# Sigmoid attention and a split-precision MLP on one core: attention issued in held groups of two pieces, with small moves at the start

## The chip, the cores and the metric

The kernel runs on one core of a Trainium2 chip. The time is device microseconds for one execution; before the change three runs gave a median of 1160.83 us (1160.44 to 1162.7). One further execution was recorded by the hardware profiler, and all durations below come from it.

## The reference, cut to what matters

```python
scores = q @ k.T / sqrt(64) - log(448)          # 8 batches x 12 heads, 448 x 448
x = (1 / (1 + exp(-scores))) @ v                # sigmoid attention, no row sum
x = x.transpose(0, 2, 1, 3).reshape(3584, 768)
h = x @ w_in                                    # 768 -> 2048
g = where(h >= 1, h, where(h <= -1, 0, (h + 1) ** 2 / 4))
out = g @ w_out                                 # 2048 -> 768
```

q, k and v are float32, the two weights float64.

## The kernel before, in words

**Precision.** Nearly every product is done with float16 halves: an operand is scaled by a power of two and split into a high half (ACT, or POOL) and a low half (DVE, or POOL: what the high half missed), and three matmuls add high x high, low x high and high x low in PSUM. The first eight pairs of heads go through in plain float32 instead.

**Attention.** The unit is a pair of heads (6 pairs a batch, 48 in all), and a pair has four pieces: three of 128 keys and a middle one with the last 64 keys of both heads (`NPC` pieces, piece number `i`, pair `p`, place `c`). A piece has two halves. `scores` makes the scores of some pieces in PSUM tiles `psc` (two buffers, `ps_sc`): for float16 pairs two full-array matmuls on 128 rows per piece (L409), then two matmuls on 64 rows each, one for each head, which the array runs at the same time in its two row halves (L418). The middle piece of pairs 14 and later has three full-array matmuls in their place (L404). `weigh` then takes the sigmoid on ACT (L447 for the first 14 pairs, L450 later) and splits it into halves `ahl` on ACT (L458) and DVE (L459). `av` multiplies by v (L491): each matmul fills 64 columns, one head each, and two run at the same time in the array's two column halves; a piece has six of them, a middle one four. So three ways of dividing the array alternate on PE: whole, two row halves (scores' second part), two column halves (av).

**The MLP.** `up` (batches 0 and 1, L719) and `up_blocks` (later batches, L685, with seven block products from pre-mixed weights) make h; `bend` does the activation on ACT and DVE; `down` (L755) makes the output. All are full-array matmuls. They are emitted as a list of units, and `step(i)`, which emits pieces of attention of the next batch, is called between units at even shares, so attention of batch b+1 lies among the MLP of batch b. `step` emits the scores some pieces ahead and then `av`: one piece at a time for pairs before 14, and from pair 14 on two pieces at every even place.

**What sets the order.** The program is written in that order, but only SP's queue keeps it. On the other engines a scheduler moves instructions: it takes the ready instruction of the highest priority by its own estimate, so two matmuls of one piece may end up apart with MLP matmuls between them. PE works strictly through the order that comes out.

**The start.** SP loads pair 0 (L307: q and k in one transfer, L308: v), then a chunk of w_in (L210), and so on. Until about 67 us PE does the float32 attention of pairs 0 to 7 while ACT (L236) and DVE convert the sixteen chunks of w_in. `find_scale` at step 12 finds the scale of the first eight chunks; `split(0)` and `split(1)` (L277 on ACT, L280 on DVE) follow at once, `split(2)` and `split(3)` after batch 0's x is done. `prep_a` (largest values, L335) and `prep_b` (halves, L366 and L367, and their transfers L380/L381) prepare the first two float16 pairs, 8 and 9, at steps 19 and 22, 20 and 23. `all_sum` (L155) is a tiny matmul that adds up largest values for the preparation two pairs ahead.

Of the kernel before, what the change touches and what calls it, by code (L numbers as in the profile page):

```python
# [14 lines left out]
F32 = mybir.dt.float32  # L15
# [23 lines left out]
WI_A = 12  # L39
WO_A = 42  # L40
# [15 lines left out]
CORN = 10  # L56
TP = 1
# [12 lines left out]
def sigmoid_attention_mlp(ctx: ExitStack, tc: tile.TileContext, first_qvk, qkv, w_in, w_out, out_t):  # L70
# [117 lines left out]
    class Weight:  # L188
# [84 lines left out]
        def split(self, f):  # L273
# [4 lines left out]
            if self is wi and f > AHEAD:  # L278
                behind(ins, "g")
# [22 lines left out]
    def load_pair(p):  # L302
        if p >= NPAIR or not first_time("load", p):
            return
        if p < NFULL:
            r = full[:, slot_of(p)]
            nc.sync.dma_start(out=r[:, ::2, :], in_=first_qvk[p, :, ::2, :])  # L307
            nc.sync.dma_start(out=r[:, 1, :], in_=first_qvk[p, :, 1, :])  # L308
            ready[p] = r, r[:, 1]
            return  # L310
# [74 lines left out]

    def scores(todo):

        tiles = []
        for i in todo:
# [5 lines left out]
            if p < NFULL:  # L395
                r = ready[p][0]
                for j in range(2):
                    out = psc[j * D : (j + 1) * D, 0, :S] if mid else psc[:, j, :S]
                    rows = slice(j * D, (j + 1) * D)
                    nc.tensor.matmul(out, r[rows, 2, w], r[rows, 0, :], start=True, stop=True)  # L400
            elif mid and p >= NFULL + NHALF:
                hl = ready[p][4]
                for t, (kh, qh) in enumerate(((0, 0), (1, 0), (0, 1))):
                    nc.tensor.matmul(psc[:, 0, :S], corner(p)[:, kh, :], hl[:, 0, qh, :], start=t == 0, stop=t == 2)  # L404
            else:
                kq = ready[p][0]
                for j in range(2):
                    out = psc[j * D : (j + 1) * D, 0, :S] if mid else psc[:, j, :S]
                    nc.tensor.matmul(out, kq[:, j, 1, w], kq[:, j, 0, :], start=True, stop=False)  # L409
        for i, psc in zip(todo, tiles):  # L410
# [8 lines left out]
            if mid and p >= NFULL + NHALF and p + 2 in maxes:  # L419

                sums[p + 2] = all_sum(maxes[p + 2], 3, psc[:, 1, :])
# [16 lines left out]
    def weigh(i, psc):  # L438
# [6 lines left out]
        if p < NFULL + NHALF:  # L445
            a32 = att_p.tile([P, 2, S], F32, tag="ahl", name="a32")
            nc.scalar.activation(a32[:, :n, :], a, AF.Sigmoid, bias=nls, scale=sqk)  # L447
# [9 lines left out]
        for x, hi, lo in parts:  # L457
            nc.scalar.activation(hi, x, AF.Copy, scale=ATT)  # L458
            nc.vector.scalar_tensor_tensor(out=lo, in0=x, scalar=ATT, in1=hi, op0=ALU.mult, op1=ALU.subtract)  # L459
# [4 lines left out]
    def av(i):  # L464
        p, c = divmod(i, NPC)
        b, hp = divmod(p, NP)
        if c == 0:
            state["pav"] = ps_av.tile([P, 512], F32, tag="pav", name="pav")
            if hp == 0:
                state["xm"] = sml_p.tile([P, NP], F32, tag="xm", name="xm", bufs=2)  # L470
        pav = state["pav"]
        at = pieces.pop(i)
        mid = c == NKC
        v = ready[p][1]
        split = p >= NFULL + NHALF
        terms = []
        for j in range(2):
            o = slice(j * D, (j + 1) * D)
            full_v = slice((2 * c + j) * D, (2 * c + j + 1) * D)
            if p < NFULL and mid:  # L480
                full_v = slice(2 * c * D, (2 * c + 1) * D)
            if not split:
# [487 lines left out]
```

## Time and profile before

| what | value |
|---|---|
| median of three runs | 1160.83 us |
| profiled execution | 1159.12 us, span of its instructions 1157.4 us |
| PE busy | 1135.0 us, 7662 matmuls |
| DVE, ACT, POOL busy | 815.8, 722.1, 294.4 us |
| granted TensorE clock | 0.999 |

The profile page lists, by engine, how long instructions were under way. A matmul's own duration overlaps that of the next (they are pipelined), so what a matmul costs PE is read from the starts: from its start to the start of the one behind it. In the timeline view like instructions in a row are merged: `start, duration, engine, line, operation, out<-in, array rows*columns, shape, count`. The field such as `64*128` names the part of the array that a matmul uses. A bracket at a row's end is the engine's idle time before it and what ended that.

### The profile page before, as it was taken

The numbers are of one execution on the slowest core, as the hardware profiler recorded it, in microseconds if no ns is written. First come the engines' busy times: TensorE is split into PE (matmuls) and PEld (weight loads), VectorE is DVE, ScalarE is ACT, GpSimd is POOL, SyncE is SP. The second block draws the span as 40 slices with busy tenths as digits, with TensorE's granted clock in tenths as the row PEclk, the third lists the DMA queues.
The fourth block names the chain that finished last, engine by engine and source line by source line (L and its number), as shares of the span: only waits on it lengthen the run. The fifth ranks groups of instructions, "written<-read, shape, count | busy, mean of one in ns | idle before, by whom it ended". The sixth has DMA issues, their size and how long they took to land.

```text
span 1157.4 us, 20215 instructions
## 1 busy us (share of the span) xinstructions
PE 1135.0 (98%) x7662; PEld 666.1 (58%) x7662; DVE 815.8 (70%) x1730; ACT 722.1 (62%) x1199; POOL 294.4 (25%) x367
## 2 busy tenths in 40 slices
PE   8899999999999999999999999999999999999998
PEld 2234334444446775567745785457854677558954
DVE  6988886879987895468936787367964589646820
ACT  6978888578666784557754786447764576423410
POOL 0000000001542354324523353325344233210000
PEclk9999999999999999999999999999999999999999
DMA  9943443162564654225632465224742165203300
GB/s 366 380 138 135 143 165 97 50 212 105 192 209 144 239 211 127 76 94 205 219 102 65 145 207 203 66 66 147 264 145 76 53 207 200 100 17 123 133 22 27
DMA packets 58112, 170.00 MB, mean 147 GB/s; under 512 B 8608, under 2 KB 39840, under 8 KB 51872
## 3 DMA queue, kind: packets, MB, share of 16 engines
q1 hardware_dynamic: 56288, 159.29, 39.9%
q10 hardware_dynamic: 1728, 9.44, 2.3%
q8 instruction: 60, 0.98, 0.3%
q14 instruction: 36, 0.29, 0.1%
HBM read 126.94 MB, written 23.40 MB: 130 GB/s over the span
## 4 chain that ended last, share of the span: by engine, by line
PE 76%; DMA 8%; DVE 6%; ACT 4%; POOL 3%; issue 1%; SPq 0%; POOLq 0%; DVEq 0%; ACTq 0%
PE po L755 30%; PE ph L685 23%; PE pav L491 8%; PE ph L719 7%; DMA raw<-qkv 4%; PE psc L409 3%; PE psc L418 3%; DMA w_out_sb<-w_in 2%; PE psc L404 1%; DVE ahl L459 1%; ACT psc L450 1%; POOL hl L373 1%; DVE mixa L625 1%; ACT dump L335 1%; POOL raw L371 1%
## 5 line engine op out<-in xcount | busy, mean ns | idle before, releaser
L755 PE MATMUL po<-ghl,w_out_sb 128*128 128x448 f16 x2304 | 446.9, 353 | 1.8 <-ACT ghl L735 1.8
L755 PEld LDWEIGHTS <-w_out_sb 128*128 128x128 f16 x2304 | 221.5, 98 | 217.2 <-issue 17.6
L685 PE MATMUL ph<-w_in_sb 128*128 128x224 f16 x3024 | 307.7, 259 | 1.7 <-DMA w_in_sb<-blocks 1.3
L685 PEld LDWEIGHTS <-w_in_sb 128*128 128x128 f16 x3024 | 282.6, 98 | 31.1 <-issue 27.6
L459 DVE SCALAR_TENSOR_TENSOR ahl<-psc,ahl 128x896 f16<-128x896 f32 (+1 forms) x170 | 153.0, 900 | 98.8 <-ACT ahl L458 96.9
L450 ACT ACTIVATE psc<-psc,nls,sqk 128x896 f32<-128x896 f32 (+1 forms) x136 | 129.8, 971 | 94.0 <-PE psc L418 76.1
L371 POOL TENSOR_SCALAR raw<-raw,qkv_s 128x448 f32<-128x448 f32 (+1 forms) x93 | 70.9, 777 | 443.8 <-DVE qkv_i L135 355.7
L458 ACT ACTIVATE ahl<-psc 128x896 f16<-128x896 f32 (+1 forms) x170 | 127.0, 762 | 30.6 <-DVE ahl L459 29.4
L719 PE MATMUL ph<-xhl,w_in_sb 128*128 128x448 f16 x576 | 112.5, 353 | 0.0
L335 ACT ACTIVATE dump<-raw 128x448 f16<-128x448 f32 (+1 forms) x105 | 61.6, 587 | 72.0 <-DMA raw<-qkv 71.3
L694 DVE TENSOR_TENSOR xhl<-ph,xhl 128x224 f32<-128x224 f32 x240 | 87.7, 383 | 26.0 <-PE ph L685 19.6
L491 PE MATMUL pav<-ahl,v 128*64 128x448 f16 x748 | 98.2, 360 | 0.4 <-DVE ahl L459 0.4
L735 ACT ACTIVATE ghl<-g 128x448 f16<-128x448 f32 x128 | 72.5, 572 | 37.2 <-DVE g L734 36.7
L732 ACT ACTIVATE g<-xhl,hr,ihr 128x448 f32<-128x448 f32 x96 | 68.7, 752 | 41.8 <-DVE xhl L694 40.8
L736 DVE TENSOR_TENSOR ghl<-g,ghl 128x448 f16<-128x448 f32 x128 | 84.2, 664 | 8.2 <-ACT ghl L735 7.7
L733 DVE SCALAR_TENSOR_TENSOR g<-g,rk 128x448 f32<-128x448 f32 x112 | 79.8, 727 | 13.9 <-ACT g L732 13.5
L719 PEld LDWEIGHTS <-w_in_sb 128*128 128x128 f16 x576 | 54.8, 98 | 58.2 <-issue 8.9
L373 POOL TENSOR_TENSOR hl<-raw,hl 128x448 f16<-128x448 f32 x62 | 72.8, 1194 | 0.0
L409 PE MATMUL psc<-qk 128*128 128x448 f16 x252 | 66.4, 354 | 2.8 <-ACT a L447 1.8
L734 DVE SCALAR_TENSOR_TENSOR g<-xhl,ihs,g 128x448 f32<-128x448 f32 x96 | 66.3, 708 | 0.3
L768 DVE TENSOR_SCALAR o<-po,od 128x448 f32<-128x448 f32 x42 | 28.5, 679 | 53.1 <-PE po L755 53.1
L430 POOL COPY w_in_sb<-hl 64x128 f16<-64x128 f16 x68 | 32.4, 476 | 127.3 <-DVE hl L367 125.4
(151 smaller groups left out, 1131.6 us busy)
## 6 DMA issues: line engine op xcount, KB each, us to landing
w_in_sb<-blocks SPq DMA_DIRECT2D x48, 1344.0 KB, 6.6
raw<-qkv SPq DMA_DIRECT2D x34, 704.0 KB, 4.8
qk<-hl SPq DMA_DIRECT2D x320, 56.0 KB, 2.0
w_out_sb<-w_in SPq DMA_DIRECT2D x16, 768.0 KB, 11.1
out_t<-o SPq DMA_DIRECT2D x48, 224.0 KB, 1.9
blocks<-mixs SPq DMA_DIRECT2D x8, 768.0 KB, 3.5
w_out_sb<-w_out ACTq DMA_DIRECT2D x6, 768.0 KB, 4.6
raww<-w_out ACTq DMA_DIRECT2D x6, 768.0 KB, 5.8
```

Of the source, the lines that this page charges most:

```text
L371: nc.gpsimd.tensor_scalar(out=rt, in0=rt, scalar1=s[:, t : t + 1], scalar2=1.0, op0=ALU.mult, op1=ALU.mult)
L373: nc.gpsimd.tensor_tensor(out=dst[:, 1, :], in0=rt, in1=hi, op=ALU.subtract)
L409: nc.tensor.matmul(out, kq[:, j, 1, w], kq[:, j, 0, :], start=True, stop=False)
L450: nc.scalar.activation(a, a, AF.Sigmoid, bias=nls, scale=sqk)
L458: nc.scalar.activation(hi, x, AF.Copy, scale=ATT)
L459: nc.vector.scalar_tensor_tensor(out=lo, in0=x, scalar=ATT, in1=hi, op0=ALU.mult, op1=ALU.subtract)
L491: nc.tensor.matmul(pav[j * D : (j + 1) * D, :S], *terms[j][t], start=c == 0 and t == 0, stop=mid and t == len(terms[j]) - 1,)
L685: nc.tensor.matmul(out, w[:, wt, wh, c * P : (c + 1) * P], xc[:, xt, c, xh, :], start=j in (0, 2) and c + wh + xh == 0, stop=c == HC - 1 a ...
L694: add = lambda out, q, other: nc.vector.tensor_tensor(out=out, in0=quarter(q), in1=other, op=ALU.add)
L719: nc.tensor.matmul(ph[:, :S], w_in_sb[:, f, wh, c * P : (c + 1) * P], xhl[:, c, xh, :], start=c == 0 and wh + xh == 0, stop=c == NCC - 1 a ...
L736: (nc.gpsimd if f % GPOOL else nc.vector).tensor_tensor(out=ghl[:, f, 1, :], in0=g, in1=hi, op=ALU.subtract)
L755: nc.tensor.matmul(po[:, :S], w_out_sb[:, f, wh, m * P : (m + 1) * P], ghl[:, f, gh, :], start=f == lo and wh + gh == 0, stop=f == hi - 1 ...
```

## The change

It has five parts.

1. **Held groups.** `weigh` notes the instructions that make a piece's operands (`made`). The first matmul of a call of `scores` now waits for those of the pieces two before (whose PSUM tiles it takes over), and the first matmul of a call of `av` waits for all the pieces of the call. Until then no matmul of that group is ready for the scheduler, and afterwards all are.
2. **Two pieces from pair 7 on.** `step` emits pieces in twos from pair 7 (`GROUPED`), not from pair 14. `av` takes the list.
3. **Order in `scores`.** The half with j=1 of L409 comes first, and `all_sum` stands between the whole-array and the row-half matmuls of the group, not behind them.
4. **The first transfer is divided.** q, then the first 128 columns of k, then the rest of k.
5. **Later splits and preparation.** `split(0)`, `split(1)` and `split(2)` come at steps 21, 23 and 24, `split(3)` after x; pair 9's preparation is left to the ordinary call at steps 28 and 30, and pair 8's `prep_b` comes at step 21.

```diff
+    made = {}
+    def when_made(some):
+        waits = [ins for i in some for ins in made.get(i, ())]
+        def once(ins):
+            while waits:
+                tc.add_manual_dep(ins.ins, waits.pop().ins.name, ...)
+        return once
     def scores(todo):
+        once = when_made(i - 2 for i in todo)
...
-                for j in range(2):
+                for j in (1, 0):
-                    nc.tensor.matmul(out, kq[:, j, 1, w], kq[:, j, 0, :], start=True, stop=False)
+                    once(nc.tensor.matmul(out, kq[:, j, 1, w], kq[:, j, 0, :], start=True, stop=False))
+        for i, psc in zip(todo, tiles):
+            p, c = divmod(i, NPC)
+            if c == NKC and p >= NFULL + NHALF and p + 2 in maxes:
+                sums[p + 2] = all_sum(maxes[p + 2], 3, psc[:, 1, :])
...
-    def av(i):
+    def av(some):
+        once = when_made(some)
+        for i in some:
...
-        if i < NPC * (NFULL + NHALF):
+        if i < NPC * GROUPED:
             more, some = i + LAG + 1, [i]
...
-            nc.sync.dma_start(out=r[:, ::2, :], in_=first_qvk[p, :, ::2, :])
+            if p == 0:
+                nc.sync.dma_start(out=r[:, 0, :], in_=first_qvk[p, :, 0, :])
+                for w in (slice(0, P), slice(P, S)):
+                    nc.sync.dma_start(out=r[:, 2, w], in_=first_qvk[p, :, 2, w])
...
-            for what, when in ((load_pair, L0), (prep_a, A0), (prep_b, A0 + 1)):
-                for k in range(2):
+            for what, when in ((load_pair, L0), (prep_a, A0), (prep_b, A0 + 2)):
+                for k in range(1 if what != load_pair else 2):
...
-                    wi.split(0)
-                    wi.split(1)
+            if at in SPLITS:
+                with tc.high_priority(offset=WI_PRIO):
+                    wi.split(SPLITS.index(at))
```

The order that the scheduler makes of it differs all along PE. PE's queue in batch 2's first block products shows how; `psc` with its number is the PSUM tile of one piece, `qk` and `hl` are the stacked and the plain halves of q and k. Before:

```order
L409 LDWEIGHTS qk_4923
L409 MATMUL psc_5328<-qk_4923 128x448
L418 LDWEIGHTS hl_4912
L418 MATMUL psc_5328<-hl_4912 128x448
L418 LDWEIGHTS hl_4912
L418 MATMUL psc_5328<-hl_4912 128x448
L409 LDWEIGHTS qk_4923
L409 MATMUL psc_5331<-qk_4923 128x448
L409 LDWEIGHTS qk_4923
L409 MATMUL psc_5331<-qk_4923 128x448
L418 LDWEIGHTS hl_4912
L418 MATMUL psc_5331<-hl_4912 128x448
```

The same two pieces after the change, whose lines L435 and L449 are L409 and L418 of before:

```order
L435 LDWEIGHTS qk_4925
L435 MATMUL psc_5333<-qk_4925 128x448
L435 LDWEIGHTS qk_4925
L435 MATMUL psc_5333<-qk_4925 128x448
L449 LDWEIGHTS hl_4914
L449 MATMUL psc_5330<-hl_4914 128x448
L449 LDWEIGHTS hl_4914
L449 MATMUL psc_5330<-hl_4914 128x448
L449 LDWEIGHTS hl_4914
L449 MATMUL psc_5333<-hl_4914 128x448
L449 LDWEIGHTS hl_4914
L449 MATMUL psc_5333<-hl_4914 128x448
```

The whole-array matmuls of both pieces now stand together, and so do the row-half ones, so that the array is divided anew once for two pieces.

ACT's queue from the first piece of pair 6 on, in the float32 attention (`a` is a piece's sigmoid, with `nls` its bias; `hl` the halves of pair 8, and with `hl,m` the largest values of pair 9). Before:

```order
L277 ACTIVATE w_in_sb<-w_in_sb,wi_s 128x768
L447 ACTIVATE a_440<-psc,nls 128x896
L335 ACTIVATE hl,m_444<-raw 128x448
L366 ACTIVATE hl<-raw,qkv_s 128x448 x2
L236 ACTIVATE w_in_sb<-w_out_sb 128x768
L335 ACTIVATE hl,m_444<-raw 128x448
L236 ACTIVATE w_in_sb<-w_out_sb 128x768
L447 ACTIVATE a_455<-psc,nls 128x896
L497 ACTIVATE x_92<-pav 128x448
L447 ACTIVATE a_488<-psc,nls 128x896
L447 ACTIVATE a_661<-psc,nls 128x448
L366 ACTIVATE hl<-raw,qkv_s 128x448 x2
```

After, where L475, L238, L376, L279 and L530 are L447, L236, L366, L277 and L497 of before:

```order
L475 ACTIVATE a_440<-psc,nls 128x896
L238 ACTIVATE w_in_sb<-w_out_sb 128x768
L376 ACTIVATE hl<-raw,qkv_s 128x448 x2
L279 ACTIVATE w_in_sb<-w_in_sb,wi_s 128x768
L475 ACTIVATE a_451<-psc,nls 128x896
L530 ACTIVATE x_92<-pav 128x448
L475 ACTIVATE a_460<-psc,nls 128x896
L279 ACTIVATE w_in_sb<-w_in_sb,wi_s 128x768
L475 ACTIVATE a_633<-psc,nls 128x448
L279 ACTIVATE w_in_sb<-w_in_sb,wi_s 128x768
L475 ACTIVATE a_660<-psc,nls 128x896
L475 ACTIVATE a_688<-psc,nls 128x896
```

Pair 9's two L335 and two L366 are gone from here, and the splits L279 stand between the sigmoids of pair 6 one by one.

SP's queue at the start (`ghl` is the buffer of the float32 pairs, `first_qvk` their data). Before:

```order
L307 DMA ghl<-first_qvk 128x2x448
L308 DMA ghl<-first_qvk 128x448
L210 DMA w_out_sb<-w_in 128x1536
L307 DMA ghl<-first_qvk 128x2x448
L308 DMA ghl<-first_qvk 128x448
```

After:

```order
L313 DMA ghl<-first_qvk 128x448
L315 DMA ghl<-first_qvk 128x128
L315 DMA ghl<-first_qvk 128x320
L318 DMA ghl<-first_qvk 128x448
L212 DMA w_out_sb<-w_in 128x1536
L317 DMA ghl<-first_qvk 128x2x448
```

Two issues more stand ahead of v, and the rest of k moves behind the first 128 columns. POOL's queue is the same in both.

More of the change, by code (lines that the diff above doesn't have):

```diff
@@ L399, in scores @@
                     rows = slice(j * D, (j + 1) * D)
-                    nc.tensor.matmul(out, r[rows, 2, w], r[rows, 0, :], start=True, stop=True)
+                    once(nc.tensor.matmul(out, r[rows, 2, w], r[rows, 0, :], start=True, stop=True))
             elif mid and p >= NFULL + NHALF:
@@ L458, in weigh @@
             nc.scalar.activation(hi, x, AF.Copy, scale=ATT)
-            nc.vector.scalar_tensor_tensor(out=lo, in0=x, scalar=ATT, in1=hi, op0=ALU.mult, op1=ALU.subtract)
+            made.setdefault(i, []).append(nc.vector.scalar_tensor_tensor(
+                out=lo, in0=x, scalar=ATT, in1=hi, op0=ALU.mult, op1=ALU.subtract
+            ))
         pieces[i] = ahl
     state = {"scored": 0}
-    def av(i):
[L465 to L482, printed above, removed]
-                r = o if mid else slice(0, P)
-                terms.append([(v[r, full_v], at[r, 0 if mid else j, :])])
-            elif mid:
-                terms.append([(v[:, vh, full_v], at[:, 0, j, :]) for vh in range(2)])
-            else:
-                terms.append([(v[:, vh, full_v], at[:, ah, j, :]) for vh, ah in ((0, 0), (1, 0), (0, 1))])
-        for t in range(len(terms[0])):
-            for j in range(2):
-                nc.tensor.matmul(
-                    pav[j * D : (j + 1) * D, :S], *terms[j][t],
-                    start=c == 0 and t == 0, stop=mid and t == len(terms[j]) - 1,
-                )
@@ new lines, in av @@
+    def av(some):
+        once = when_made(some)
+        for i in some:
+            p, c = divmod(i, NPC)
+            b, hp = divmod(p, NP)
+            if c == 0:
+                state["pav"] = ps_av.tile([P, 512], F32, tag="pav", name="pav")
+                if hp == 0:
+                    state["xm"] = sml_p.tile([P, NP], F32, tag="xm", name="xm", bufs=2)
+            pav = state["pav"]
+            at = pieces.pop(i)
+            mid = c == NKC
+            v = ready[p][1]
+            split = p >= NFULL + NHALF
+            terms = []
+            for j in range(2):
+                o = slice(j * D, (j + 1) * D)
+                full_v = slice((2 * c + j) * D, (2 * c + j + 1) * D)
+                if p < NFULL and mid:
+                    full_v = slice(2 * c * D, (2 * c + 1) * D)
+                if not split:
+                    r = o if mid else slice(0, P)
+                    terms.append([(v[r, full_v], at[r, 0 if mid else j, :])])
+                elif mid:
+                    terms.append([(v[:, vh, full_v], at[:, 0, j, :]) for vh in range(2)])
+                else:
+                    terms.append([(v[:, vh, full_v], at[:, ah, j, :]) for vh, ah in ((0, 0), (1, 0), (0, 1))])
+            for t in range(len(terms[0])):
+                for j in range(2):
+                    once(nc.tensor.matmul(
+                        pav[j * D : (j + 1) * D, :S], *terms[j][t],
+                        start=c == 0 and t == 0, stop=mid and t == len(terms[j]) - 1,
+                    ))
@@ L854, in sigmoid_attention_mlp @@
         group_scales(0, inv_x, 0)
-    wi.split(2)
-    wi.split(3)
+    for f in range(len(SPLITS), AHEAD + 1):
+        wi.split(f)
     units = ups(0) + downs(0, 0)
```

24 lines of the change are left out of this document (16 added, 8 removed).

## Prediction

> **What bounds the kernel now.** The page comes first: it says which engine has no room.
>
> ```profile
> span 1157.4 us, 20215 instructions
> PE 1135.0 (98%) x7662; PEld 666.1 (58%) x7662; DVE 815.8 (70%) x1730; ACT 722.1 (62%) x1199; POOL 294.4 (25%) x367
> ```
>
> PE is under way for all but 22 us. So either PE's waits go, or its matmuls must take less time. The list of waits on PE shows what the first can give:
>
> ```profile
> PE psc L400 <- DMA ghl<-first_qvk: 4.4, 1, 4.4
> PE psc L400 <- ACT a L447: 3.6, 6, 1.3
> PE psc L171 <- DVE diag L161: 2.1, 1, 2.1
> PE po L755 <- ACT ghl L735: 1.8, 3, 1.1
> PE psc L409 <- ACT a L447: 1.8, 3, 1.0
> ```
>
> The first two, 8 us, lie in the float32 attention ahead of 67 us; the rest are single events. The larger stock is inside "busy", and only starts show it. PE's timeline in one batch's block products:
>
> ```profile
> 500.21 1.32 PE L491 MATMUL pav<-ahl,v 128*64 128x448 f16 x12
> 501.46 6.21 PE L685 MATMUL ph<-w_in_sb 128*128 128x224 f16 x63
> 507.51 0.54 PE L409 MATMUL psc<-qk 128*128 128x448 f16 x2
> 507.99 0.36 PE L418 MATMUL psc<-hl 64*128 64x448 f16 x2
> 508.28 0.55 PE L409 MATMUL psc<-qk 128*128 128x448 f16 x2
> 508.77 0.36 PE L418 MATMUL psc<-hl 64*128 64x448 f16 x2
> 509.06 1.14 PE L491 MATMUL pav<-ahl,v 128*64 128x448 f16 x10
> 510.13 4.49 PE L685 MATMUL ph<-w_in_sb 128*128 128x224 f16 x45
> ...
> 523.92 1.89 PE L685 MATMUL ph<-w_in_sb 128*128 128x224 f16 x18
> 525.65 0.73 PE L409 MATMUL psc<-qk 128*128 128x448 f16 x3
> 526.31 0.55 PE L418 MATMUL psc<-hl 64*128 64x448 f16 x4
> 526.79 0.95 PE L491 MATMUL pav<-ahl,v 128*64 128x448 f16 x8
> ...
> 541.96 0.36 PE L418 MATMUL psc<-hl 64*128 64x448 f16 x1
> 542.26 1.90 PE L685 MATMUL ph<-w_in_sb 128*128 128x224 f16 x18
> ```
>
> The field 128\*128, 64\*128 or 128\*64 says how the array is divided. I read four prices from start to start.
>
> - Six pairs of L491 take 501.46 - 500.21 = 1.25 us, five take 510.13 - 509.06 = 1.07. One pair more is 0.18 to 0.19 (I use 0.19), so a run of L491 costs 0.12 us beside its pairs, until what is behind it starts.
> - Two L418 side by side take 508.28 - 507.99 = 0.29, two such pairs 526.79 - 526.31 = 0.48: 0.19 a pair and 0.10 a run.
> - A single L418 takes 542.26 - 541.96 = 0.30, as much as two: a pair that is torn apart pays its 0.19 twice.
> - Going over from the whole array to a divided one: two L409 take 507.99 - 507.51 = 0.48 ahead of L418, and three take 526.31 - 525.65 = 0.66. Three at 0.19 are 0.57, two are 0.38; so about 0.10 is the change. Where the array stays whole nothing is added: 18 L685 take 525.65 - 523.92 = 1.73, or 0.096 each, with L409 behind them.
>
> So each change of the array's division costs PE about 0.1 us that shows as busy, not as idle.
>
> [...]
>
> **The change part by part.** *Held groups, pieces in twos, the order in scores* act as one: they decide how often PE's queue changes its division. I counted that in the order of both programs; the held first matmul makes it come out so, since all of a group becomes ready at once.
>
> - Runs of float16 L491: 126 before (48 of odd length, each with a torn pair's half), 86 after (16 odd). 40 runs fewer by 0.12 is 4.8 us; 16 pairs mended (32 odd runs fewer, two to a pair) by 0.19 is 3.0.
> - Runs of L418: 122 (20 of one matmul) to 91 (2 of one). 31 by 0.10 is 3.2; 9 pairs mended by 0.19 is 1.7.
> - Entries from the whole array into a divided one: 178 to 95. 83 by 0.096 is 8.0.
>
> Together 20.7 us: 4.8 of them before the first block product, 15.9 in batches 2 to 6. The float32 part hardly changes (99 changes of division with a float32 side before, 97 after), and I put it at nothing. PE has no other work to hide these under, and it waits for nobody meanwhile, so each is on the path.
>
> *The moved `all_sum`* is inside that count: it stood behind L418 and made the array whole once more. *The reversed j* moves no cost: the same two matmuls in the other order; if it cost anything it would be one 0.10 per scores group at most, and the rows have no sign of it.
>
> *What holding adds.* The waiting instruction is the first matmul of a group, and PE takes its queue in order: all MLP matmuls behind it wait too, then `bend` on ACT and DVE. What is the cover? In the new order 63 to 81 L685 or some 40 to 50 L755 stand between groups; in the block products the shortest way is a run of 12 L491 (1.25) and 63 L685 (6.05), 7.3 us from the last L418 to the next scores. What is needed: the second piece's low half, which frees its PSUM tile.
>
> ```profile
> 531.25 1.08 DVE L459 SCALAR_TENSOR_TENSOR ahl<-psc,ahl 128x896 f16<-128x896 f32 x1
> ```
>
> Its piece was in the run of four L418 that ended at 526.31 + 0.55 = 526.86, and the row ends at 532.33: 5.5 us. That leaves 1.8 us. But ACT and DVE are not empty there:
>
> ```profile
> 140.00:160.00 20.00, 19.36 (x102) 8.38 (x101) 18.83 (x39) 18.47 (x29) 0.00 (x0) 1.00 0.42 122
> 501.00:573.00 72.00, 72.00 (x645) 55.40 (x642) 60.25 (x129) 56.83 (x102) 33.07 (x41) 1.00 0.54 189
> ```
>
> (PE, PEld, DVE, ACT, POOL busy.) DVE has 60.25 of 72 us in the block products and 18.83 of 20 at 140 us. Bounds: nothing, if the margin holds everywhere; 12 us, if one group in each of nine loaded places (five batches, four in batches 0 and 1) waits as long as the longest wait for a sigmoid above, 1.3. I take 2.5, since before's tight order paid singles of 1.0 to 2.1.
>
> *The first transfer.* The timeline's first issues on SP, and PE's first row:
>
> ```profile
> 0.79 0.43 SPq L307 DMA_DIRECT2D ghl<-first_qvk  x1
> 1.29 0.45 SPq L308 DMA_DIRECT2D ghl<-first_qvk  x1
> 4.44 1.12 PE L400 MATMUL psc<-ghl 64*128 64x448 f32 x2 [4.44 <-DMA ghl<-first_qvk]
> ```
>
> The page's part on DMA issues has a small transfer beside it (KB each, us to landing):
>
> ```profile
> qk<-hl SPq DMA_DIRECT2D x320, 56.0 KB, 2.0
> ```
>
> From issue to first matmul 448 KB took 3.65 us. Now 224 + 64 KB suffice, but the second of them is issued 0.50 later. At the 2.0 us of the small transfers in the last row it lands at 3.3, a gain of 1.1; at 3.65 again it lands at 4.94, a loss of 0.5. I take a gain of 0.6, nearer to the small one since only 64 KB are late. v and w_in are issued two slots (1.0 us) later; PE does not wait for either in the rows of before.
>
> *Later splits, later pair 9.* They leave ACT in the stretch in which it is full:
>
> ```profile
> 50.00:60.00 10.00, 6.72 (x30) 1.93 (x31) 9.15 (x22) 10.00 (x17) 0.00 (x0) 1.00 0.75 268
> ```
>
> PE's waits in it:
>
> ```profile
> 51.37 1.02 PE L400 MATMUL psc<-ghl 64*128 64x448 f32 x4 [0.95 <-ACT a L447]
> ...
> 56.85 0.16 PE L155 MATMUL pm<-mb,one 128*128 128x2 bf16 x1 [0.75 <-DVE mb L152]
> 58.34 0.97 PE L400 MATMUL psc<-ghl 64*64 64x448 f32 x4 [1.32 <-ACT a L447]
> ```
>
> And what ACT does in it:
>
> ```profile
> 51.74 0.93 ACT L277 ACTIVATE w_in_sb<-w_in_sb,wi_s 128x768 f16<-128x768 f32 x1
> ...
> 53.46 0.57 ACT L335 ACTIVATE hl<-raw 128x448 f16<-128x448 f32 x1
> 53.92 0.20 ACT L335 ACTIVATION_READ_ACCUMULATOR hl<-raw 128x1 f32 x1
> 54.02 1.22 ACT L366 ACTIVATE hl<-raw,qkv_s 128x448 f16<-128x448 f32 x2
> ```
>
> ACT is busy all 10 us and PE waits 0.95 + 0.75 + 1.32 = 3.0. Pair 9's preparation leaves the stretch: two L335 (0.77 each) and two L366 (1.22) are 2.8 us, and its tiny L155, for which PE waited 0.75, goes too. Two or three splits of 0.93 come in, one between sigmoids. Net ACT has 1 to 2 us less. Bounds: 3.0 gained, or nothing; I take 1.5. The same work comes back on ACT, DVE and SP (eight transfers, 4 to 5 us of SP's issuing) after 70 us, under MLP matmuls; pair 9's first scores stand behind 198 L719 (0.19 each, 37 us), so nothing waits for it.
>
> Sum: -20.7 - 0.6 - 1.5 + 2.5 = -20.3. The profiled execution, 1159.12 us, would be 1138.8; the median of the runs lay 1.7 above it, and from 1160.83 the forecast is **1140.5**.
>
> **The rivals.**
>
> *Half is lost where ACT and DVE are loaded.* The saving lies mostly among block products (DVE 84%) and in batches 0 and 1 (94% at 140 us). If those engines, not PE, set the pace there, PE finishes sooner and waits. For it: the 140 us row. Against it: 84% leaves 11 us of a 72 us stretch, and about 3 are saved in it. Half of 20.7 gone gives 1151.
>
> *The held heads stall PE: slower.* Before, a group's first matmuls could start with one piece ready; now the whole queue stands until the second is. It decides at 22.8 / 91 = 0.25 us for each held scores run. At 0.5, half the longest wait of L409 for a sigmoid (1.0), it costs 45 us: 1183. Against it: the margin of 1.8 us, and before's order, made by the same scheduler with splits as tight, waited little. [...]
>
> *The gaps are not PE's.* If the 0.1 us is how the profiler places starts, grouping gives nothing and only the start gains: 1160.83 - 2.1 + 2.5 = 1161. Against it: the sums of starts are the elapsed time itself.
>
> **How the numbers follow.** Forecast 0.65 (its own range 1136 to 1146: 1160.83 less 20.7, 1.1 and 3.0 is 1136.0; with 5 more of waiting 1145.5). Half lost 0.25, around 1146 to 1155. Slower 0.05. No gain 0.05, within 0.2% (2.3 us, about what a measurement can tell) or just beyond: 0.03 same, 0.02 faster. The range for 8 in 10 is 1136 to 1152: most of the forecast and rather more than half of the second. Faster 0.92, same 0.03, slower 0.05.
>
> **What would show it.** Right: in the timeline of the block products, L418 in runs of four, L491 in runs of 10 and 12, at the same prices; the groups' PE waits on L459's successor under 5 us in all; the stretch to 67 us some 2 us shorter; each batch of block products and output some 3 us shorter than its 138. Wrong: PE rows with brackets at the heads of scores groups (then it is a rival above), or runs as long as forecast with a period that does not shrink.

## The result, and the profile after

The changed kernel takes 1178.32 us (median of four runs, 1178.15 to 1178.9) against 1160.63 for the kernel before beside it (four runs, 1159.01 to 1162.7): 1.0152 times as long, 95% interval 1.0135 to 1.017. The forecast was 1140.5, so the sign was wrong. The profiled execution took 1178.28 us. Its page:

```profile
span 1176.4 us, 20214 instructions
PE 1123.5 (96%) x7662; PEld 672.0 (57%) x7662; DVE 813.2 (69%) x1730; ACT 722.9 (61%) x1199; POOL 289.3 (25%) x367
```

PE's busy time fell by 11.5 us, and the span grew by 19.0. So the work did get cheaper, and PE now stands idle for 53 us where it stood for 22. The list of waits on PE says for what:

```profile
PE ph L718 <- DVE xhl L727: 16.6, 8, 5.7
PE po L788 <- ACT ghl L768: 6.3, 4, 2.7
PE psc L435 <- DVE ahl L487: 5.5, 4, 2.7
PE psc L426 <- DMA ghl<-first_qvk: 3.5, 1, 3.5
PE psc L426 <- ACT a L475: 3.4, 5, 1.3
```

(L718, L788, L435 and L426 are L685, L755, L409 and L400 of before; L727 frees a `ph` tile, L768 and L487 are the high half of `g` and the low half of a piece.) The two longest entries are not at the heads of the held groups. They are MLP matmuls that wait for DVE and ACT.

Did the runs and prices come out as forecast? PE's timeline in batch 3's block products:

```profile
520.41 6.21 PE L718 MATMUL ph<-w_in_sb 128*128 128x224 f16 x63
...
547.22 0.92 PE L435 MATMUL psc<-qk 128*128 128x448 f16 x4
548.08 0.55 PE L449 MATMUL psc<-hl 64*128 64x448 f16 x4
548.56 1.14 PE L524 MATMUL pav<-ahl,v 128*64 128x448 f16 x10
549.62 4.68 PE L718 MATMUL ph<-w_in_sb 128*128 128x224 f16 x47
555.95 2.94 PE L718 MATMUL ph<-w_in_sb 128*128 128x224 f16 x29 [1.64 <-DVE xhl L727]
```

They did: four L449 take 548.56 - 548.08 = 0.48, ten L524 take 1.06, and the groups stand together. I took every matmul's time to the next start, less the idle time before that, and added them up by kind, for both kernels. Float16 L491 (now L524) went from 90.2 to 83.1 us, L418 from 38.8 to 33.9, L409 from 56.7 to 53.0, L404 from 21.3 to 20.0. These 17.0 us are measured. The changes of division behind MLP runs go from 4.1 to 1.6 us if each costs the 0.095 of the prediction's row, so that part is priced and not measured. Together 19.5 us were saved, where 20.7 were forecast. Against it stand idle time +31.1, MLP matmuls +6.2, float32 attention +2.0, and the first wait -0.9: together 19 us longer. Of the 6.2, some 2.4 come from a granted clock of 0.50 behind two waits (last section). Most of the rest belongs to the waits too: the last MLP matmul ahead of a wait counts with its whole duration, since no next one overlaps it (an L718 is under way 0.26 us where starts lie 0.096 apart, an L788 0.35 where they lie 0.19 apart), and there are 32 of them in place of 8.

Where it happens is best seen by stages, cut at four matmuls: the first of `up`, and the first block product of batches 2, 3 and 6 (us, profiled executions; the last column ends at the last L755's start).

| kernel | to first `up` | to batch 2's products | batch 2 | batches 3 to 5 | rest |
|---|---|---|---|---|---|
| before | 66.8 | 297.1 | 137.6 | 413.6 | 238.3 |
| after | 65.6 | 303.4 | 151.4 | 413.2 | 238.7 |

Three things need a cause: +6.3 ahead of the block products, +13.8 in batch 2, and no gain at all in batches 3 to 5, where some 3 us per batch were saved.

The loss of batch 2 begins with the longest wait. PE's timeline there, after:

```profile
368.98 5.35 PE L718 MATMUL ph<-w_in_sb 128*128 128x224 f16 x54
379.98 1.84 PE L718 MATMUL ph<-w_in_sb 128*128 128x224 f16 x9 [5.65 <-DVE xhl L727]
381.61 0.95 PE L435 MATMUL psc<-qk 128*128 128x448 f16 x2
```

ACT's timeline in that wait:

```profile
369.97 1.65 ACT L478 ACTIVATE psc<-psc,nls,sqk 128x448 f32<-128x448 f32 x2
375.59 0.58 ACT L345 ACTIVATE dump<-raw 128x448 f16<-128x448 f32 x1 [3.97 <-DMA raw<-qkv]
...
376.17 1.32 ACT L486 ACTIVATE ahl<-psc 128x896 f16<-128x896 f32 x2
...
377.95 0.34 ACT L730 ACTIVATE xhl<-ph 128x224 f32<-128x224 f32 x1
```

L345 is L335 of before, ACT's pass over `raw` from which a pair's scales are taken. It stands (ACT is idle at the head of its queue) 3.97 us for a load. Behind it in ACT's queue are the halves of a pair already scored (L486). DVE's timeline has their low halves and L727 behind those:

```profile
377.10 1.09 DVE L487 SCALAR_TENSOR_TENSOR ahl<-psc,ahl 128x896 f16<-128x896 f32 x1 [2.92 <-ACT ahl L486]
...
378.89 0.62 DVE L487 SCALAR_TENSOR_TENSOR ahl<-psc,ahl 64x448 f16<-64x448 f32 x1
379.53 0.39 DVE L727 TENSOR_TENSOR xhl<-ph,xhl 128x224 f32<-128x224 f32 x1
```

L727 ends at 379.92, and PE starts at 379.98. SP's queue shows a part of why the load is late:

```profile
358.06 0.47 SPq L390 DMA_DIRECT2D qk<-hl  x1
...
364.34 0.53 SPq L694 DMA_DIRECT2D w_in_sb<-blocks  x1
...
365.92 0.64 SPq L329 DMA_DIRECT2D raw<-qkv  x1
```

It is issued at 365.92, behind another pair's transfers and a load of block weights, and ACT gets it at 375.59. How much of the lateness is that place in the queue, run e7 tests.

In these rows ACT took L486 only behind L345, though what it reads was there: the sigmoids had ended at 371.62, and it began at 376.17, 4.55 us later, when L345 had run.

### The profile page after: what moved, and what is told of

The parts are those of the page before. It is cut to its first block, busy times and chain, and to the rows that moved or that the text cites. A ratio compares the mean times of both kernels' runs of the same rounds, so it can differ in the third digit from the quotient of the medians.

```text
span 1176.4 us, 20214 instructions
## 1 busy us (share of the span) xinstructions
PE 1123.5 (96%) x7662; PEld 672.0 (57%) x7662; DVE 813.2 (69%) x1730; ACT 722.9 (61%) x1199; POOL 289.3 (25%) x367
## 4 chain that ended last, share of the span: by engine, by line
PE 48%; DVE 16%; ACT 14%; DMA 9%; issue 5%; POOL 5%; SPq 2%; POOLq 0%; DVEq 0%; ACTq 0%
PE po L788 24%; PE ph L718 9%; PE ph L752 6%; DMA raw<-qkv 5%; PE pav L524 5%; DVE ahl L487 4%; ACT psc L478 4%; DVE xhl L727 3%; ACT ahl L486 2%; DVE g L766 2%; PE psc L435 2%; DVE g L767 2%; DMA w_out_sb<-w_in 2%; ACT ghl L768 2%; ACT dump L345 2%
## 5 line engine op out<-in xcount | busy, mean ns | idle before, releaser
L788 PE MATMUL po<-ghl,w_out_sb 128*128 128x448 f16 x2304 | 445.4, 353 | 7.7 <-ACT ghl L768 6.3
L788 PEld LDWEIGHTS <-w_out_sb 128*128 128x128 f16 x2304 | 222.6, 98 | 223.0 <-issue 21.0
L718 PE MATMUL ph<-w_in_sb 128*128 128x224 f16 x3024 | 302.6, 260 | 19.9 <-DVE xhl L727 16.6
L718 PEld LDWEIGHTS <-w_in_sb 128*128 128x128 f16 x3024 | 287.4, 98 | 38.6 <-issue 35.4
L487 DVE SCALAR_TENSOR_TENSOR ahl<-psc,ahl 128x896 f16<-128x896 f32 (+1 forms) x170 | 153.1, 901 | 100.1 <-ACT ahl L486 98.3
L381 POOL TENSOR_SCALAR raw<-raw,qkv_s 128x448 f32<-128x448 f32 (+1 forms) x93 | 75.7, 827 | 455.2 <-DVE qkv_i L137 395.9
L486 ACT ACTIVATE ahl<-psc 128x896 f16<-128x896 f32 (+1 forms) x170 | 125.9, 763 | 38.4 <-DVE ahl L487 37.3
L345 ACT ACTIVATE dump<-raw 128x448 f16<-128x448 f32 (+1 forms) x105 | 61.9, 589 | 88.7 <-DMA raw<-qkv 87.6
L768 ACT ACTIVATE ghl<-g 128x448 f16<-128x448 f32 x128 | 73.0, 573 | 59.7 <-DVE g L767 58.9
L727 DVE TENSOR_TENSOR xhl<-ph,xhl 128x224 f32<-128x224 f32 x240 | 87.1, 384 | 18.0 <-PE ph L718 12.8
L752 PEld LDWEIGHTS <-w_in_sb 128*128 128x128 f16 x576 | 55.1, 98 | 62.9 <-issue 11.1
L524 PE MATMUL pav<-ahl,v 128*64 128x448 f16 x748 | 88.0, 360 | 0.0
L435 PE MATMUL psc<-qk 128*128 128x448 f16 x252 | 62.5, 357 | 8.8 <-DVE ahl L487 5.5
L383 POOL TENSOR_TENSOR hl<-raw,hl 128x448 f16<-128x448 f32 x62 | 67.7, 1112 | 0.0
L767 DVE SCALAR_TENSOR_TENSOR g<-xhl,ihs,g 128x448 f32<-128x448 f32 x96 | 66.8, 708 | 0.3
L458 POOL COPY w_in_sb<-hl 64x128 f16<-64x128 f16 x68 | 27.9, 411 | 142.2 <-DVE hl L377 140.2
```

The lines of the kernel that those rows point to most:

```text
L435: once(nc.tensor.matmul(out, kq[:, j, 1, w], kq[:, j, 0, :], start=True, stop=False))
L487: made.setdefault(i, []).append(nc.vector.scalar_tensor_tensor(out=lo, in0=x, scalar=ATT, in1=hi, op0=ALU.mult, op1=ALU.subtract))
L524: once(nc.tensor.matmul(pav[j * D : (j + 1) * D, :S], *terms[j][t], start=c == 0 and t == 0, stop=mid and t == len(terms[j]) - 1,))
L718: nc.tensor.matmul(out, w[:, wt, wh, c * P : (c + 1) * P], xc[:, xt, c, xh, :], start=j in (0, 2) and c + wh + xh == 0, stop=c == HC - 1 a ...
L727: add = lambda out, q, other: nc.vector.tensor_tensor(out=out, in0=quarter(q), in1=other, op=ALU.add)
L752: nc.tensor.matmul(ph[:, :S], w_in_sb[:, f, wh, c * P : (c + 1) * P], xhl[:, c, xh, :], start=c == 0 and wh + xh == 0, stop=c == NCC - 1 a ...
```

## The experiments

Before each expectation stands the edit; every time is a median beside runs of the kernel before on the same chip, the ratio is to those.

### Which part of the change loses what

**e1_no_hold** takes the holding away.

```diff
-        waits = [ins for i in some for ins in made.get(i, ())]
+        waits = []
```

> The changed kernel without the held waits (twos from pair 7, the order in scores, the divided transfer and the later splits stay). Theory A (the holding makes the waits: PE's queue stands at the head of a group while ACT and DVE work through what is ahead of the group's operands): the 45 us of gaps fall back to about 14, and most of the saving goes too, since the order has 482 changes of division against 515 before and 361 after: 1155 to 1160 us. Rival B (twos from pair 7 put batch 2's attention later, holding or not): the 380 us and 412 us gaps stay, 1170 or more. Rival C (the moved splits and pair 9 do it): 1175 or more.

1165.16 us, ratio 1.0044 (1.0029 to 1.0059). Batch 2 takes 137.4 us: its whole loss went with the holding. But the kernel is above theory A's range, and the stage ahead of batch 2 still takes 304.4: something else is lost there.

**e2_group14** is the changed kernel with `GROUPED = 14`.

> The changed kernel with pieces in twos from pair 14 only, as before the change; the holding stays. Theory A: the loss ahead of the first block product shrinks a little (single pieces have less to wait for), the 5.65 us gap at 380 us and those behind it stay, as do the periodic ones: 1172 to 1179. Rival B (twos): back to 1150 to 1160, since the loss of 5 us by the first block product and the 10 us behind it are gone while most of the saving by fewer changes stays.

1173.18, ratio 1.0113 (1.0095 to 1.0131). Batch 2 takes 144.9, half its loss, and the stage ahead of it 303.0. The twos from pair 7 are not the cause, but single pieces up to pair 14 soften it.

**e3_start** is the kernel before with the divided transfer, the later splits and the later pair 9 alone.

> The kernel before with two parts of the change alone: the divided first transfer, and the later splits and pair 9. All that the change does at the start is in it. Theory A and rival B: 1 to 2 us less than before by 66 us and nothing lost later: 1158.5 to 1160. Rival C (pair 9's preparation and the splits come later and push batch 1's and 2's preparation back): some of the 15 us loss up to batch 2's block products is here: 1165 to 1178.

1164.56, ratio 1.0045 (1.003 to 1.0059): the changes at the start cost 5 us by themselves, which rival C came nearest to, though at less than its price. All of it lies ahead of batch 2 (303.0 against 297.1), most between 67 and 187 us. Its PE timeline there:

```profile
107.23 0.97 PE L500 MATMUL pav<-a,v 128*64 128x448 f32 x2
108.13 3.96 PE L728 MATMUL ph<-xhl,w_in_sb 128*128 128x448 f16 x20
...
120.45 0.54 PE L418 MATMUL psc<-qk 128*128 128x448 f16 x2 [0.99 <-ACT a L456]
```

and the kernel before's in the same work:

```profile
104.60 0.97 PE L491 MATMUL pav<-a,v 128*64 128x448 f32 x4
105.51 0.55 PE L409 MATMUL psc<-qk 128*128 128x448 f16 x2
```

Before, four float32 matmuls, two and two side by side, take 0.91 us; here two alone take 0.90, since their partners stand elsewhere. A torn float32 pair costs 0.45, and the stage has five or six of them (+2.6 us), beside 2.5 us more of waits.

**e4_hold_b3** holds only from batch 3's attention on, with `GROUPED = 14`.

> The changed kernel with the holding from batch 3's attention on only, and twos from pair 14; the start parts stay. Theory A: the loss up to 501 us (the holding in batches 1 and 2) is gone, and behind it fewer changes and the periodic waits cancel, as they do after the change (each period 137.7 against 137.1): 1157 to 1161. If instead each held head costs the same wherever it stands, half or more of the 17.7 us loss stays: 1168 or more.

1164.76, ratio 1.0043 (1.0027 to 1.0059), above theory A's range. Batch 2 takes 137.9, all later stages what they took before, and 303.7 are ahead of batch 2, as in e3 (303.0), which the range left out. In batches 3 to 5 the holding gains nothing (413.8 against 413.6).

**e5_no_start** is the changed kernel with the start of before.

> The changed kernel with the start of before: first transfer whole, splits and pair 9 where they were; holding and twos from pair 7 stay. The two start parts alone cost 5 us (run e3_start), holding from batch 3 on nothing beyond that (e4_hold_b3). Theory A (the parts add up: start 5, holding in batches 1 and 2 the rest): 1172 to 1174. Rival (the loss of batch 2 needs the later pair 9, since a preparation that is late once stays late): 1160 to 1166.

1175.74, ratio 1.0129 (1.0103 to 1.0155), 1.7 above theory A's range and far from the rival's: 302.6 ahead of batch 2, 150.9 in it. So the holding and the twos from pair 7, which this run does not tell apart, lose 5.5 us ahead of batch 2 without the start parts as well, and the two losses there do not add up. Batch 2's loss does not need the later pair 9.

**e8_pair9_early** is e3 with pair 9's preparation back in its place; the same lines put pair 8's `prep_b` one step earlier, as before the change.

```diff
-            for what, when in ((load_pair, L0), (prep_a, A0), (prep_b, A0 + 2)):
-                for k in range(1 if what != load_pair else 2):
+            for what, when in ((load_pair, L0), (prep_a, A0), (prep_b, A0 + 1)):
+                for k in range(2):
```

> The start parts of run e3_start (kernel before, divided transfer, later splits), but pair 9's preparation where it was. Theory A (it is pair 9's later preparation that costs the 5 us between 67 and 187 us: its scores wait for ACT and a transfer, and float32 pairs of av are torn apart round it): 1158.5 to 1160. Rival (the later splits cost it): 1163 to 1165.

1160.96, ratio 1.0003 (0.9991 to 1.0015), 1 us above theory A's range and equal to the kernel before beside it (1160.31). The later preparation, pair 9's above all, was what cost some 4 us; divided transfer and later splits come to nothing that can be measured.

### Is it ACT, standing for raw?

**e7_late_set** issues two loads of block weights later, so that one no longer stands ahead of the late load of raw.

```diff
-                if b == 1 and u == last - 2:
-                    for n in range(3):
+                if b == 1 and u in (last - 2, last + 12):
+                    for n in (0,) if u < last else (1, 2):
```

> The changed kernel with the second and third load of block weights issued 14 units later, so that one of them no longer stands ahead of a load of raw on SP and no longer shares the DMA engines with it; PE's order is the same. Theory A (the 5.65 us gap at 380 us is ACT standing 3.97 us for that raw at L345 with the halves of a held pair behind it): the load lands 2 to 6 us sooner, the gap shrinks by as much, and half clock behind it goes too: 1172 to 1176. Rival (the gap is the held pair's own work on ACT and DVE): within 1 us of the changed kernel, 1178.

1175.58, ratio 1.0141 (1.0126 to 1.0157). By time it can't be told from the changed kernel. In the profile the 5.65 us wait is 4.38 and batch 2 takes 148.8 in place of 151.4. That is the direction of theory A, but 1.3 us off the wait where it gave 2 to 6, so the place in SP's queue is only a part of the lateness, and this run does not decide between the two.

**e9_no_max** and **e11_before_no_max** leave ACT's pass over raw out for pairs 14 and later, in the changed kernel and in the kernel before.

```diff
-            if p < MAX_ACT:
+            if p < NFULL + NHALF:
...
+            if p >= NFULL + NHALF:
+                nc.gpsimd.memset(m, 4.0)
```

> The changed kernel without L345 for pairs 14 and later: their largest values are not computed (a constant stands in their place), so ACT has some 2.3 us less per pair and never stands for a load of raw. Leaves that part of the computation out. Theory C (PE's saved time comes back as waits because ACT, in order, stands for raw or works through two pieces' sigmoids, halves and largest values at once, and with it DVE and the MLP tiles): the 45 us of gaps fall to 15 to 25, and the time to 1148 to 1162, well below the same edit of the kernel before (run e11). Rival D (DVE or the pieces' own chain from scores to halves is what PE waits for): gaps stay near 40, 1172 to 1178.

> The kernel before with the same edit as run e9, as a control: largest values of pairs 14 and later not computed. It has 14 us of gaps in all, of which 4.4 are the first wait and some 6 lie ahead of pair 14; so by every theory at most 4 us are gained here: 1155 to 1161.

1153.1, ratio 0.9951 (0.9935 to 0.9966), and 1149.36, ratio 0.9914 (0.9896 to 0.9933). The distance between the two kernels shrinks from 17.7 us to 3.7. But the control gained 10 where I allowed 4, and e9 is not below it: the pass weighs on the kernel before too. In the profiled executions PE has 3.3 us less idle time there, and the other 5.7 are its own time, in an order with 475 changes of division in place of 515.

**e10_max_nowait** and **e12_before_nowait** keep the pass on ACT but let it read what lies in SBUF anyway.

```diff
+                    if n == 3:
+                        rt, to = w_out_sb[:, 0, 0, : rt.shape[1]], spare
```

> The changed kernel in which L345 of pairs 14 and later reads data that lies in SBUF anyway in place of raw (its results are not used, a constant stands in their place): ACT has the same number of L345 but never waits for a load of raw. Leaves the true largest values out. If the standing for raw is what costs (theory C, first half): the 5.65 us gap at 380 us and the L788 waits for L768 go, 1158 to 1168. If ACT's work is what costs (second half): the ends are near run e9 only without L345, and here 1172 to 1178.

> Control for run e10: the kernel before, in which L335 of pairs 14 and later reads data that lies in SBUF in place of raw, its results unused and a constant in their place. Leaves the true sums over raw out. Theory C (the standing for raw costs because a held group's work is queued behind it): the kernel before gains little, mostly by the order (496 changes against 515): 1155 to 1158, so the distance of 17.7 us to the changed kernel shrinks to 5 to 8. Rival E (the standing costs both alike): 1144 to 1147.

1163.26, ratio 1.004 (1.0028 to 1.0052), and 1155.39, ratio 0.996 (0.9948 to 0.9973). Both times are as theory C had them. Against the runs of before beside them (1159.0 and 1159.81) the changed kernel is 4.3 us slower in place of 17.7, and the kernel before 4.4 faster: the same work on ACT without the standing is worth 13 us to the one and 4.4 to the other, and the distance between them is 8.7, a little more than the 5 to 8 of the expectation. PE's timeline of e10 at the place of the longest wait:

```profile
372.34 1.02 PE L723 MATMUL ph<-w_in_sb 128*128 128x224 f16 x9 [0.20 <-DVE xhl L732]
374.09 0.55 PE L440 MATMUL psc<-qk 128*128 128x448 f16 x2 [0.72 <-DVE ahl L492]
```

From the first `up` to the end of batch 2, e10 takes 441.5 us. With the start parts and no holding in those batches it is 440.9 (e3) or 441.6 (e4), in the changed kernel 454.8. So in sum the holding costs nothing there beyond the start parts once ACT does not stand for raw. (Against its own control, e12 with 434.1, e10 loses 7.3; e3 loses 6.2 against the kernel before, 434.7. In batch 2 alone e10 still takes 141.5.)

**e14_before_dve** and **e15_dve** do the pass on DVE (`MAX_ACT = 14`), and **e13_av_dve** does so with only `av` held, twos from pair 14, and of the start parts only the divided transfer.

> The kernel before with that pass on DVE from pair 14 on, nothing else. The order has 508 changes, the prices give 4 us. Theory C: 1153 to 1158. Rival D: 1159 to 1165.

> The changed kernel with that pass on DVE from pair 14 on. If it was ACT in particular that must not stand: 1158 to 1166, as in run e10. If any in-order engine that stands for raw does the harm (DVE has L487 and L727 behind it): 1170 to 1178.

> Only av held, twos from pair 14, the first transfer divided, splits and pair 9 as before; and the pass over raw for the scales of pairs 14 and later is on DVE (a true largest value, 2 instructions a pair) in place of ACT's L345. The order has 431 changes (515 before); by the prices of the prediction that is 13 us. Theory C (ACT's queue is what ate the saving): 1148 to 1154, faster than both kernels. Rival D (DVE is as full, and stands for raw in ACT's place): 1158 or more.

1174.81, ratio 1.0126 (1.0106 to 1.0146); 1182.06, ratio 1.02 (1.0176 to 1.0224); 1178.58, ratio 1.0167 (1.0115 to 1.0219). The first two are worse than I gave for either side; e13, whose four runs lie between 1173 and 1186, falls in rival D's open range. The waits on DVE in e14:

```profile
DVE ahl L459 <- ACT ahl L458: 89.0, 27, 7.5
DVE o L768 <- PE po L755: 49.7, 12, 8.4
DVE m L339 <- DMA raw<-qkv: 33.7, 20, 5.1
```

DVE now stands for raw 20 times, and has 55 us more to do (871.4 busy against 815.8); the kernel before, without any holding, loses 15 us by the two, which these runs do not tell apart. So ACT is the better place for the pass here, and it is not only a held order that suffers when an engine that frees PSUM for PE is late: in e14 PE's L685 waits 7.1 us for DVE's L694 (11 times), in the kernel before 0.4 (once).

**e16_pass_behind**, **e17_behind_first** (the same with splits and pair 9 of before) and **e18_before_behind** (the same in the kernel before) keep the whole computation, and put the pass behind the halves of the group just scored.

```diff
-            if late:
-                prep_a(p + 3)
...
+                    elif n == 3 and t == 0 and "half" in latest:
+                        behind(ins, "half")
...
+        if c == 2 and late:
+            prep_a(p + 3)
```

> The changed kernel, whole computation, with one thing moved: the pass over raw on ACT (L345 of pairs 14 and later) stands in ACT's queue behind the halves (L486) of the group just scored, not ahead of them. The order keeps its few changes (362), and batch 1's end comes after 513 matmuls of L788 in place of 553. Theory C (the place of L345 ahead of the halves costs): the 5.65 us gap goes, 1160 to 1167, as in run e10 where L345 did not wait. If the held waits themselves cost: 1174 to 1180.

> Run e16's kernel with the splits and pair 9 as before; only the divided transfer stays of the start parts. By run e8 against e3 pair 9 costs 3.6 us, with the splits 4: 1156 to 1163; if it comes out below 1158 it beats both kernels.

> The kernel before with the pass over raw behind the halves, as a control. Its order is about as divided as before (526 changes against 515), and its PE waits little for ACT; theory C: 1155 to 1160. If the pass's place costs the kernel before as much, as in the runs without it: 1145 to 1152.

1169.87, ratio 1.009 (1.0068 to 1.0111); 1166.92, ratio 1.0067 (1.0046 to 1.0088); 1161.36, ratio 1.002 (1.0008 to 1.0031). e16 lies between the two theories, e17 3.9 us above my range, and e18 1.4 above theory C's: it gains nothing. Batch 2 takes 136.8 us in e16, its loss is gone; but the stage ahead of it takes 314.2, 10.8 more than in the changed kernel, and e17's 311.1. PE's timeline of e16 in batch 1:

```profile
300.64 3.58 PE L754 MATMUL ph<-xhl,w_in_sb 128*128 128x448 f16 x18
310.52 0.93 PE L437 MATMUL psc<-qk 128*128 128x448 f16 x2 [6.30 <-DVE ahl L489]
```

Here a held head itself stands: the order put only 18 matmuls of `up` between two groups, and the low half that the second waits for came 6.3 us after them. That is the rival of the prediction that was given 0.05, in another kernel. Of the 10.8 us, 5.1 are more idle time (18.8 against 13.7 in that stage), and some 6 are lost at a granted clock of 0.50, about half of that behind this wait:

```profile
306.34:316.58 10.24, 6.06 (x24) 2.16 (x25) 10.24 (x17) 8.13 (x17) 3.03 (x4) 0.50 0.80 285
```

(A window's length, then PE, PEld, DVE, ACT and POOL busy, granted clock, DMA share and GB/s. PE works 6.06 us in it at half clock; two more such windows, 3.4 us each, begin at 139.09 and 279.03.)

### Is it the held scores?

**e6_av_held** holds only the calls of `av`, with twos from pair 14 and the start of before.

```diff
-        once = when_made(i - 2 for i in todo)
+        once = when_made(())
```

> Only the calls of av are held, not those of scores; twos from pair 14, start of before. The order has 443 changes of division (515 before), runs of L491 of 9, 10 and 12, and batch 1's end stands after 508 matmuls of L788 (488 before, 553 in the changed kernel). Theory A (what costs is the held scores: two pieces' scores at once give ACT and DVE two pieces' work at once, and MLP tiles come free late behind it; priced saving here 10 us): 1149 to 1155. Rival (any holding makes the waits): 1160 to 1172.

1160.38, ratio 1.0004 (0.9994 to 1.0014). Theory A falls in this form: the time lies at the lower end of the rival's range. In its profiled execution, counted as above, 10.4 us of PE's time were saved, and 8.9 of idle time, 2.1 of MLP and 1.2 of float32 matmuls came in (the mean granted clock was 0.997, in the kernel before 0.999). Yet e5 differs from this run only by the held scores and the twos from pair 7, and is 15 us slower, with 14 of them in batch 2 (150.9 against 136.6). So the held scores with the twos make the loss; holding `av` alone neither loses nor gains.

### What is left in batches 3 to 5

The window of one whole batch (its length, then PE, PEld, DVE, ACT and POOL busy). After:

```profile
520.40:657.90 137.50, 134.23 (x1023) 89.19 (x1021) 91.41 (x201) 86.86 (x152) 52.85 (x68) 1.00 0.42 141
```

Before:

```profile
501.50:638.50 137.00, 137.00 (x1023) 88.45 (x1021) 94.84 (x213) 86.62 (x152) 54.12 (x68) 1.00 0.42 143
```

Before, PE is busy for all of it; after, it has 2.8 us less to do and stands for 3.3. Two waits come in every batch. One is at 555.95 in the timeline above, behind a run of four L435 and four L449. DVE's timeline round it:

```profile
553.67 1.09 DVE L487 SCALAR_TENSOR_TENSOR ahl<-psc,ahl 128x896 f16<-128x896 f32 x1 [0.18 <-ACT ahl L486]
554.68 0.61 DVE L769 TENSOR_TENSOR ghl<-g,ghl 128x448 f16<-128x448 f32 x1
555.21 0.68 DVE L727 TENSOR_TENSOR xhl<-ph,xhl 128x224 f32<-128x224 f32 x2
555.81 1.08 DVE L487 SCALAR_TENSOR_TENSOR ahl<-psc,ahl 128x896 f16<-128x896 f32 x1
```

ACT has no idle time from 549.04 to 558; two sigmoids, two halves, the pass over raw and the activation of `g` all come at once, since two pieces were scored at once. The other, 1.24 us at 604.29, has ACT standing for raw again:

```profile
603.10 0.58 ACT L345 ACTIVATE dump<-raw 128x448 f16<-128x448 f32 x1 [3.59 <-DMA raw<-qkv]
...
603.68 0.56 ACT L768 ACTIVATE ghl<-g 128x448 f16<-128x448 f32 x1
```

Without the standing, batches 3 to 5 take 409.6 us held (e10) and 409.6 not held (e12); without the pass 405.3 (e9) and 408.0 (e11). So the holding is worth 0 to 3 us there, of the 8 to 9 by which PE's own time is shorter in the changed kernel. e10 still has 2.6 us of waits in each batch, e12 none.

## Why the prediction was wrong

**The term that carried it was right.** Fewer changes of the array's division saved 19.5 us of PE's time, forecast 20.7, at the prices read from before; 2.5 of it are priced by the prediction's own row. (Of its terms, 31 runs at 0.10 are 3.1 and not 3.2, which changes nothing.)

**The step that failed is "What holding adds"**, +2.5 with bounds 0 and 12. In its place came 31.1 us more idle time and 6.2 on MLP matmuls, with float32 attention a further 2.0; the start parts by themselves lose some 5 of the whole (e3). The step measured PE's matmuls against one chain, scores to low half, at one place in the block products, and asked only when the head of the next group can start. That chain was a small part: L435's waits for L487 are 5.5 us in all. Its length was also read from before, at 5.5 us; in the changed kernel's batch 3 it takes 8.3, from 548.08 + 0.55 to 555.81 + 1.08, more than the cover of 7.3. The step left two things out. The first is who else is in ACT's and DVE's queues: the MLP's tiles come free there, behind both pieces of a group. The second was in the profile of before, in a view that the prediction did not read, the waits on ACT:

```profile
ACT psc L450 <- PE psc L418: 76.1, 35, 7.5
ACT dump L335 <- DMA raw<-qkv: 71.3, 14, 8.5
```

ACT stood 71 us for raw, up to 8.5 at a time, and PE hardly waited (0.2 us in all of batch 2), so what was queued behind had slack. The held order used that slack up. The same row in the changed kernel:

```profile
ACT dump L345 <- DMA raw<-qkv: 87.6, 18, 8.8
```

Up to the end of batch 2 taking the standing away is worth 13 us (454.8 against 441.5) where in the kernel before it is worth 0.6 (434.7 against 434.1).

**"PE has no other work to hide these under, and it waits for nobody, so each is on the path"** holds for PE as it was. It does not follow that all of a saving stays when PE gets shorter: a batch went from 137.0 us with PE busy throughout to 137.5 with 3.3 of waits.

**The rivals.** "Half is lost where ACT and DVE are loaded" named the right engines and had 0.25; in batches 3 to 5 not half but all is lost. "The held heads stall PE" had the sign and the wrong place: in the changed kernel mostly MLP matmuls wait, not the heads. Where a head does stand, at 338.30, PE is idle for 2.67 us, and the L788 behind it, whose `ghl` was written by 303.1, start only at 340.91. The clock has no term in the forecast; in the changed kernel the granted clock was 0.50 from 378.40 us on, inside the wait of 5.65, and from 412.53 on, just behind one of 2.35, which cost some 4 us.

**The start.** The first transfer was forecast at -0.6 and its wait went from 4.44 to 3.54. The splits and pair 9 were forecast at -1.5; pair 9 costs some 4 (e3 against e8). The failed step is "nothing waits for it": it counted the matmuls ahead of pair 9's scores, and neither what the later order does to pairs of float32 matmuls nor the waits at 120 and 153 us. Also "the float32 part hardly changes" counted changes of division, not torn pairs, which cost 0.45 each.

**What stays open.** Every edit lets the scheduler write all queues anew, so no run changes one wait alone: that e16 loses 10.8 us in batch 1 where it gained in batch 2 is seen, why the order left so little between those groups is not settled. Nor is why the start's loss and that of the holding with the twos ahead of batch 2 (5.9 and 5.5) give 6.3 together. In batches 3 to 5 the cause of the waits is read from the rows; only the part of the standing was tested. A third buffer for raw, which might take the standing away with the whole computation kept, was not tried. No version with the whole computation beat the kernel before; e6 and e8 equal it.

## What to carry to other kernels

Before pricing a saving on the engine that is busy throughout, read the waits of the engines that free its buffers: a wait there that costs nothing today is slack (here 71.3 us of ACT for raw), and a tighter order can spend it. In the held order, work that stands for a load did harm in ACT's queue ahead of work that frees PSUM (3.97 us of standing ahead of a 5.65 us wait of PE); but moving it behind (e16) took that loss away and brought another, so the whole queue has to be looked at again. And grouping work on one engine delivers it in lumps to the next (two pieces at once left ACT no idle time from 549.04 to 558), so the cover has to be worked out for everything queued behind the lump, not for the lump's own chain.

## What the runs showed of the hardware

PE's matmuls ran at half rate behind some waits and not behind others. Windows of the changed kernel round four waits (a window's length, PE's busy time behind it, and as the third number from the end the granted clock):

```profile
334.03:337.44 3.41, 1.59 (x9) 0.60 (x7) 3.41 (x5) 0.86 (x2) 1.59 (x3) 1.00 0.56 117
337.44:340.86 3.42, 2.56 (x20) 1.20 (x20) 3.25 (x4) 1.70 (x4) 0.00 (x0) 1.00 0.58 228
...
374.99:378.40 3.41, 0.00 (x0) 0.00 (x0) 1.30 (x4) 2.81 (x8) 0.00 (x0) 1.00 0.10 38
378.40:385.22 6.82, 5.24 (x24) 2.44 (x24) 4.14 (x21) 2.94 (x7) 2.73 (x5) 0.50 0.01 2
...
409.12:412.53 3.41, 1.06 (x12) 0.90 (x10) 3.41 (x6) 2.13 (x6) 2.87 (x4) 1.00 0.58 149
412.53:415.94 3.41, 3.41 (x19) 2.70 (x19) 2.31 (x6) 0.49 (x3) 0.00 (x0) 0.50 0.63 216
...
460.31:463.73 3.42, 1.67 (x16) 0.79 (x15) 0.47 (x1) 0.28 (x1) 0.00 (x0) 1.00 0.92 344
463.73:467.14 3.41, 2.38 (x12) 1.16 (x12) 0.80 (x2) 3.38 (x9) 0.00 (x0) 1.00 0.59 236
```

The waits end at 338.30, 379.98, 412.44 and 464.64 and took 2.67, 5.65, 2.35 and 2.66 us. PE's timeline behind the third:

```profile
412.44 3.46 PE L718 MATMUL ph<-w_in_sb 128*128 128x224 f16 x18 [2.35 <-DVE xhl L727]
415.69 0.68 PE L435 MATMUL psc<-qk 128*128 128x448 f16 x2
```

Eighteen L718 take 3.25 us, 0.181 each, and the nine behind the wait of 5.65 take 1.63, as much each; at a granted clock of 1.00 the 63 at 520.41 take 0.096 each. PE worked 5.24 and 3.41 us at a granted clock of 0.50, which costs some 4 us. Behind the first and the last wait the granted clock stays 1.00.

So the length of a wait does not decide alone here: the clock fell in the wait of 5.65 us and just behind the one of 2.35, and at neither of the two of 2.67 and 2.66, which are longer than 2.35. The two stretches at 0.50 last 6.82 and 3.41 us and begin 34.13 us apart. The other windows above are cut from their edges in steps of 3.41 us; that step is my choice. Ahead of the two stretches PE is busy for 0.00 and 1.06 us of such a window; in the windows in which the waits of 2.67 and 2.66 begin it is busy for 1.59 and 1.67. Four waits of one trace show no limit, and what the clock follows is not settled by these runs.
